# A two-layer decode kernel: spacing of the MLP steps, 24 instead of 48 streamed copies, evictions split evenly

## The chip, the cores and the metric

The kernel runs on one core of a Trainium2 chip. The metric is the device time of one execution in microseconds (us), lower is better. PE is the matmul engine (TensorE), with PEld its weight loads; DVE is VectorE, ACT is ScalarE, POOL is GpSimd. "Clock" is the TensorE clock that the throttle granted, as a share of full speed; the records show it at 1.0 or 0.5, and means in between.

## The reference, cut to what matters

Four blocks run in turn on 8 rows (batch 8, one token each, D = 448): attention, MLP, attention, MLP. Both attention blocks read the same K and V caches.

```
k_cache, v_cache: (8 rows, 8 kv heads, 4096, 256) bf16;  16 query heads
x = x + attention(layernorm(x))      # softmax(q k^T / 16) v, then @ wo (4096 x 448)
x = x + B(layernorm(x))              # x1 = x + ...; x1 + gelu(layernorm(x1) @ w3) @ w4
... the same two once more, same weights
```

With one token a row, the shifted convolution inside B reads only padding, so w1 and w2 drop out. What remains is 480 MB of loads, nearly all K and V (the kernel keeps the transposed K of four of a row's eight heads from layer 0 to layer 1), and little arithmetic on each byte.

## The kernel before

One row's layer 1 can start only when its layer 0 and the small dense work between (output projection, layernorm, w3, gelu, w4, layernorm, new queries: here "the MLP") are done. So the kernel interleaves: attention heads go one after the other, and the MLP of the row that has just finished layer 0 is cut into steps which are put between the attention pieces. A Python generator yields once per step. 47 of a row's 70 steps issue matmuls (8 or 7 of them); the other 23 issue a few tiny VectorE operations, or nothing.

```
def pump():                                   # called at every slot
    credit["n"] = credit["n"] + credit["rate"] if jobs else 0.0     # rate 0.8
    while credit["n"] >= 1.0:
        credit["n"] -= 1.0
        step()                                # next(jobs[0])

def mix(lo, n, then_q, ...):                  # one row: n = 1
    for c in range(KC):
        for t in range(0, 32, 8):
            outputs(lo, n, c, range(t, t + 8), t == 0, True)   # c = 0 has 64-wide weights
            yield                             # 16 TensorE steps
    yield from layernorm(...)                 # 7 steps, VectorE
    scaled(lnT, r_ln, 1, n)
    ...
    yield
    yield
    for t in range(0, NF, 2):
        project(w3_cols, w3_r, C_H, t, t + 2, n)
        yield                                 # 7 TensorE steps
    ...                                       # gelu 3, w4 8 TensorE steps, then queries:
                                              # layernorm 7, two empty, 16 TensorE steps, copy to qT
```

A head that streams K calls `turn(f)` eight times (4 transposes of 128x128 f32 on PE into one PSUM bank, then an eviction of 128x512 on DVE or ACT), `score(f)` eight times (8 matmuls, K as the weight), and multiplies by V twice (16 matmuls each). There is a slot after each turn, six of the scores and each V half: 16 slots a head. Between the end of a row's layer 0 and its layer 1 lie 95 slots; what is left by then is issued at once (`drain`).

```
# a projection with one vector (n = 1) streams it repeated, 48 columns wide:
def copies(cols, n):
    return cols.unsqueeze(1).to_broadcast([cols.shape[0], 2 * N_REP // n, n])   # N_REP = 24
ON_ACT = (2, 5, 7)                # of the eight evictions of a head, these go to ScalarE
```

K and V come in chunks of 1 MiB through a ring of 5 slots (K half, K half, V half, V half of the head before). PE frees a K half after four turns, so a late PE leaves the DMA queue without a free slot.

## Time and profile before

| | before |
|---|---|
| time | 1244.03 us (1243.63 to 1244.42, 2 runs) |
| PE busy, PEld busy | 81%, 72% |
| DVE, ACT busy | 544 us, 269 us |
| mean clock | 0.912 |
| loaded | 480 MB, 386 GB/s over the span |

The first fence has lines of the profile page: the span, PE's busy time, and the rows of 40 equal slices (clock in tenths, GB/s).

```profile
span 1245.7 us, 42311 instructions
...
PE 1008.9 (81%) x19176; PEld 894.5 (72%) x19176; DVE 544.1 (44%) x1785; ACT 268.8 (22%) x811; POOL 105.5 (8%) x281
...
PEclk9888998899988998899888999899888998999995
...
GB/s 351 382 415 419 389 383 399 416 384 389 406 414 420 336 385 409 412 389 385 399 417 416 364 387 420 416 384 367 417 412 386 385 398 413 418 381 375 394 391 89
```

DMA reaches 415 to 420 GB/s in some slices and falls below 390 in others, in every row's period. The view by windows shows one such place, where a row's MLP steps begin (head at 399). The columns are each engine's busy us (instructions), then clock, DMA share, GB/s.

```profile
core 0: us, PE busy (x) PEld busy (x) DVE busy (x) ACT busy (x) POOL busy (x), PEclk, DMA share, GB/s
395.00:400.00 5.00, 1.54 (x21) 1.22 (x22) 0.67 (x3) 0.76 (x4) 0.61 (x2) 0.81 1.02 421
400.00:405.00 5.00, 5.00 (x42) 4.17 (x41) 1.69 (x5) 0.59 (x1) 0.00 (x0) 0.50 1.00 415
405.00:410.00 5.00, 5.00 (x78) 4.75 (x78) 1.34 (x2) 0.59 (x1) 0.00 (x0) 0.67 0.77 279
410.00:415.00 5.00, 5.00 (x117) 4.38 (x116) 1.63 (x6) 1.17 (x5) 0.36 (x1) 1.00 0.57 182
415.00:420.00 5.00, 5.00 (x97) 4.93 (x96) 3.19 (x9) 1.35 (x4) 0.48 (x2) 1.00 0.99 372
```

PE is mostly idle up to 399 (1.54 us busy of 5), then all of each window is busy, at half clock at first; from 405 on the loads starve (279 and 182 GB/s). That the ring is full then is read from the code.

Two pieces of the timeline of PE (start us, span us, what), both at full clock, show what a step costs.

```profile
545.64 0.50 PE L428 MATMUL mm<-oT,wo_sb 128*128 128x48 bf16 x8
545.98 0.62 PE L562 MATMUL tk<-ident,ring 128*128 128x128 f32 x4
...
1195.09 0.34 PE L476 MATMUL mm<-hT,w_sb 128*128 128x42 bf16 x7
1195.27 0.36 PE L586 MATMUL ps<-qT,ktr 128*128 128x48 bf16 x8
```

From the start of a step to the start of what follows: 8 matmuls that stream one element 48 times take 0.34 us (42 ns each); 7 that stream 7 different elements, 42 columns in all, take 0.18 us (26 ns each).

Last, three of PE's waits for DVE (us in total, times, longest us): for the layernorm result (lnT, or t, which follows it), and for the new queries.

```profile
PE mm L399 <- DVE lnT L372: 8.1, 10, 3.0
PE mm L399 <- DVE t L372: 5.0, 1, 5.0
PE ps L586 <- DVE qT L415: 0.7, 1, 0.7
```

About 5.0 and 3.0 us of these are waits at the very end and the very start.

### The profile page before, as it was taken

To read this page: it belongs to the slowest core of one execution; us is meant where nothing else is said; L and a number is where in the kernel's file an instruction comes from. 1 tells how busy PE (TensorE), PEld (TensorE's weight loads), DVE (VectorE), ACT (ScalarE), POOL (GpSimd) and SP (SyncE) were. 2 spreads that over 40 slices of the span, in tenths; PEclk is the share of its full clock that TensorE was granted. 3 is DMA by queue.
4 is the path that set the end of the run, shared out by engine and by line. 5 is a ranking of instruction groups with operands and counts; after the bars stand their busy time and mean duration, and the time that the engine had idled before them with its cause. 6 is when DMAs were issued, how large, how long until landed. Compare 5 with 4: busy or idle time off the path is not lost.

```text
span 1245.7 us, 42311 instructions
## 1 busy us (share of the span) xinstructions
PE 1008.9 (81%) x19176; PEld 894.5 (72%) x19176; DVE 544.1 (44%) x1785; ACT 268.8 (22%) x811; POOL 105.5 (8%) x281
## 2 busy tenths in 40 slices
PE   4577897788877897788877887889778888789785
PEld 4567786677766886677766876778677877688674
DVE  3334553346333453345334543445333643445352
ACT  0222222222222221222221222222222222212120
POOL 0000000000010000100110010000100000000100
PEclk9888998899988998899888999899888998999995
DMA  9999999999999899999999999999999999999992
GB/s 351 382 415 419 389 383 399 416 384 389 406 414 420 336 385 409 412 389 385 399 417 416 364 387 420 416 384 367 417 412 386 385 398 413 418 381 375 394 391 89
DMA packets 71668, 483.06 MB, mean 388 GB/s; under 512 B 7344, under 2 KB 13248, under 8 KB 13696
## 3 DMA queue, kind: packets, MB, share of 16 engines
q1 hardware_dynamic: 71488, 480.36, 96.3%
q8 instruction: 150, 2.46, 0.8%
q14 instruction: 30, 0.25, 0.0%
HBM read 480.32 MB, written 0.01 MB: 386 GB/s over the span
## 4 chain that ended last, share of the span: by engine, by line
PE 52%; DMA 32%; DVE 11%; issue 4%; POOL 1%; ACT 0%; SPq 0%; POOLq 0%; DVEq 0%; ACTq 0%
DMA ring<-in_A_k_cache_dram 30%; PE tk L562 25%; PE ps L586 9%; PE mm L399 6%; PE mm L428 4%; PE pvb L656 3%; DVE ktr L569 3%; DMA ring<-in_A_v_cache_dram 2%; PE mm L476 2%; PE pvb L674 2%; DVE sm L333 1%; DVE sm L334 1%; DVE sm L351 1%; POOL gm L632 1%; DVE sm L332 1%
## 5 line engine op out<-in xcount | busy, mean ns | idle before, releaser
L562 PE MATMUL tk<-ident,ring 128*128 128x128 f32 x3072 | 531.0, 306 | 113.1 <-DMA ring<-in_A_k_cache_dram 111.4
L562 PEld LDWEIGHTS tk<-ident,ring 128*128 128x128 f32 x3072 | 377.0, 156 | 136.1 <-DMA ring<-in_A_k_cache_dram 129.8
L569 DVE COPY ktr<-tk 128x512 f32<-128x512 f32 x320 | 218.1, 689 | 209.0 <-PE tk L562 207.3
L656 PE MATMUL pvb<-ring,pT 128*2 128x256 bf16 x4096 | 158.2, 274 | 53.2 <-DMA ring<-in_A_v_cache_dram 49.5
L567 ACT COPY ktr<-tk 128x512 f32<-128x512 f32 x192 | 112.5, 586 | 367.9 <-PE tk L562 367.9
L586 PE MATMUL ps<-qT,ktr 128*128 128x48 bf16 x4096 | 178.1, 184 | 14.3 <-DVE ktr L569 11.8
L586 PEld LDWEIGHTS ps<-qT,ktr 128*128 128x128 bf16 x4096 | 156.4, 97 | 32.0 <-DVE ktr L569 19.0
L569 DVE COPY keep<-tk 128x512 f32<-128x512 f32 x160 | 109.8, 691 | 149.8 <-PE tk L562 149.6
L586 PEld LDWEIGHTS ps<-qT,keep 128*128 128x128 bf16 x4096 | 149.5, 99 | 26.0 <-issue 19.7
L586 PE MATMUL ps<-qT,keep 128*128 128x48 bf16 x4096 | 159.5, 186 | 6.2 <-issue 5.3
L638 ACT ACTIVATE pT<-ps,nb 128x32 bf16<-128x32 f32 x256 | 76.7, 300 | 296.0 <-DVE nb L634 283.9
L656 PEld LDWEIGHTS pvb<-ring,pT 128*2 128x2 bf16 x4096 | 74.7, 82 | 81.1 <-DMA ring<-in_A_v_cache_dram 60.7
L632 POOL PARTITION_ALL_REDUCE gm<-pm x128 | 45.7, 357 | 873.2 <-DVE pm L629 873.2
L567 ACT COPY keep<-tk 128x512 f32<-128x512 f32 x96 | 56.3, 587 | 272.7 <-PE tk L562 272.7
L629 DVE TENSOR_REDUCE pm<-ps 128x2 f32<-128x64 f32 x128 | 28.7, 224 | 143.7 <-PE ps L586 143.7
L662 DVE COPY ob<-pvb 128x256 f32<-128x256 f32 x128 | 53.9, 421 | 60.1 <-PE pvb L656 60.0
L428 PE MATMUL mm<-oT,wo_sb 128*128 128x48 bf16 (+5 forms) x1280 | 77.6, 203 | 1.9 <-DVE oT L681 1.9
L399 PE MATMUL mm<-lnT,wq_sb 128*128 128x48 bf16 x1152 | 69.1, 205 | 7.5 <-DVE lnT L372 7.5
L428 PEld LDWEIGHTS mm<-oT,wo_sb 128*128 128x128 bf16 (+1 forms) x1280 | 62.9, 105 | 12.5 <-issue 6.1
L674 PE MATMUL pvb<-ident,ob 128*128 128x128 f32 x256 | 60.3, 323 | 11.8 <-DVE ob L662 11.7
L399 PEld LDWEIGHTS mm<-lnT,wq_sb 128*128 128x128 bf16 x1152 | 55.9, 99 | 13.8 <-DVE lnT L372 9.6
L643 POOL PARTITION_ALL_REDUCE dn<-rs x128 | 51.3, 401 | 151.5 <-ACT pT L638 151.5
(59 smaller groups left out, 402.5 us busy)
## 6 DMA issues: line engine op xcount, KB each, us to landing
ring<-in_A_v_cache_dram SPq DMA_DIRECT2D x256, 1024.0 KB, 9.7
ring<-in_A_k_cache_dram SPq DMA_DIRECT2D x192, 1024.0 KB, 9.5
wo_sb<-in_A_wo_dram SPq DMA_DIRECT2D x1, 3584.0 KB, 23.0
wq_sb<-in_A_wq_dram SPq DMA_DIRECT2D x3, 1024.0 KB, 14.6
w_sb<-in_B_w_dram SPq DMA_DIRECT2D x1, 1568.0 KB, 20.6
w_sb<-in_B_w_dram SPq DMA_DIRECT2D x3, 448.0 KB, 16.5
wq_sb<-in_A_wq_dram SPq DMA_DIRECT2D x1, 512.0 KB, 11.3
w_sb<-in_B_w_dram SPq DMA_DIRECT2D x1, 224.0 KB, 16.1
```

What stands on the lines that cost most here:

```text
L399: last = e.matmul(room(P, at + t * B, n), cols(kc, t), copies(lnT[:, kc, 0:n], n), start=(kc == 0), stop=(kc == KC - 1), skip_group_check= ...
L428: last = e.matmul(room(w, at, n) if alone else mm[0:w, at:at + n], wo[:, t, row0(c):row0(c) + w], copies(cols, n) if alone else cols, star ...
L562: last = e.transpose(bank[:, j * P:(j + 1) * P], src[:, 4 * (f % 4) + j, :].bitcast(f32), ident4[:, :])
L567: op("act", lambda e: e.copy(flat, bank[:, :]), reads=[r_bank], writes=[r_kt])
L569: op("dve", lambda e: e.tensor_copy(flat, bank[:, :]), reads=[r_bank], writes=[r_kt])
L586: last = e.matmul(pst[:, at:at + 2 * N_REP].rearrange("p (r j) -> p r j", j=2), kt(i, c), repeated(qT[:, b, c, 2 * h:2 * h + 2]), start=(c ...
L632: op("pool", lambda e: e.partition_all_reduce(gm[q][0][:, :], pm[q][0][:, :], P, ReduceOp.max), reads=[pm[q][1]], writes=[gm[q][1]])
L638: return e.activation(pT[q][0][:, :, :].rearrange("p i j -> p j i")[:, j, :], pst[:, C_S:C_S + 2 * NI].rearrange("p (i j) -> p j i", j=2)[ ...
L643: op("pool", lambda e: e.partition_all_reduce(dn[q][0][:, :], rs[q][0][:, :], P, ReduceOp.add), reads=[rs[q][1]], writes=[dn[q][1]])
L656: last = e.matmul(pvb[at:at + 2, 0:DH], pT[q][0][:, a * HALF + i, :], v[:, i, :], start=(a == 0 and i < 4), stop=(a == 1 and i >= HALF - 4 ...
L662: op("dve", lambda e: e.tensor_copy(ob[:, :], pvb[:, 0:DH]), reads=[r_pv], writes=[r_ob])
L674: last = e.transpose(pvb[:, DH + c * P:DH + (c + 1) * P], ob[:, c * P:(c + 1) * P], ident4[:, :])
```

## The change

Its intent: spread a row's MLP steps over all 95 slots, with steps that cost PE time further apart than steps that don't; make the repeated vector half as wide; give ScalarE half the evictions.

```
+N_MLP = 24
 def copies(cols, n):
-    return cols.unsqueeze(1).to_broadcast([cols.shape[0], 2 * N_REP // n, n])
+    return cols.unsqueeze(1).to_broadcast([cols.shape[0], N_MLP // n, n])
 def room(w, at, n):
-    r = 2 * N_REP // n
+    r = N_MLP // n
 ...
     def step():
         if jobs:
+            n = len(S.ops["pe"])
             try:
                 next(jobs[0])
             except StopIteration:
                 jobs.pop(0)
+            return 1.0 if len(S.ops["pe"]) > n else 0.4
+        return 1.0
 
     def pump():
-        credit["n"] = credit["n"] + credit["rate"] if jobs else 0.0
-        while credit["n"] >= 1.0:
-            credit["n"] -= 1.0
-            step()
+        credit["n"] = min(1.0, credit["n"] + credit["rate"]) if jobs else 0.0
+        if credit["n"] > 0.0:
+            credit["n"] -= step()
 ...
-    ON_ACT = (2, 5, 7)
+    ON_ACT = (1, 3, 5, 7)
 ...
-            credit["rate"] = 0.8
+            credit["rate"] = 0.62
```

Stepping through both rules by hand for the 70 steps (P a TensorE step, d another, . an empty slot) gives these slots:

```
before .PPPP.PPPP.PPPP.PPPP.dddd.dddd.dPPP.PPPP.dddP.PPPP.PPPd.dddd.dddd.dPPP.PPPP.PPPP.PPPP.Pd
after  PP.PP.P.PP.PP.P.PP.PP.P.PdddddddddPPP.PP.P.PdddPPP.P.PP.PP.ddddddddddPPP.PP.P.PP.PP.P.PP.PP.P.d
```

## The prediction

> **What bounds it now.** The DMA queue table shows 480 MB; at the best rate that 5 us windows hold for long (I use 420 GB/s) that is 1144 us, and some 21 us of tail follow (timeline: attention ends at 1225, the span at 1245.7). So about 75 us are lost transfer. A row's period is 140 us (chain of waits: 249.7, 386.3, 528.1), though its 52 chunks of 1 MiB need 130. DMA's busy share (0.96) hides it; the GB/s column shows it. In the windows of one row it sags while that row's MLP steps run, 402 to 463 us: 279 and 182 GB/s at 405-415, 328 to 359 at 430-440, 445-450 and 455-460; from 465 to 545 it is 401 to 426 but for one window of 346. In most of the sagging windows PE is 5.0 of 5.0 busy: ring slots come free late.
>
> **PE's account.** Warm, a streamed head takes PE about 6.9 us without MLP steps (454.75 to 464.39 less 8 steps); its 4 chunks take DMA 10.0 us. An MLP step of 8 matmuls, one vector in 48 copies, takes 0.34 us (42 ns each) in the timeline; at 0.8 steps in each of 16 slots that is 4.35 us, 11.2 in all: over 10. Each row begins cold (granted clock 0.50, 0.67 in 400-410): a step takes 0.56 us, a transpose group 0.85 to 1.04.
>
> **What the change does.**
> 1. 24 copies: the scores (48 columns in pairs) run at about 26 to 32 ns a matmul, and the MLP steps with 7 distinct columns (42 wide) at 0.18 us for 7, 26 ns. So one repeated element seems to stream slowly, and 24 should reach that floor: about 0.21 us a step (estimate). The Trainium skill, "TensorE: Matmul & The Clock Gate", "Back-to-back issue gap", gives one floor of about 25 ns for 1 to 64 columns; the trace agrees for pairs and not for the single repeated element. 47 TensorE steps a row: about 6 us less PE.
> 2. Spacing: TensorE steps fall from 0.8 to 0.62 per slot; the others stay near one. By my count 70 steps need 88 slots before and 95 after, and 95 are there, so nothing is left to drain. MLP load per head: 16 x 0.62 x 0.21 = 2.1 us, 9.0 in all: under 10.
> 3. Evictions: DVE loses one of eight (689 ns) and ACT gains one (586 ns); they alternate. DVE waits in a row's layernorm stretch shrink; perhaps 1 us a row.
>
> **How much is critical.** Warm, PE no longer exceeds DMA; the cold start of each row (about 4.5 us of lost transfer in 405-415) shrinks to about 2. I expect 3 of the 10 us lost per row to stay: 7 x 7.5 rows is about 52 us, less 1 to 2 us in the tail.
>
> **Predicted: 1193 us, 8 in 10 within 1174 to 1217.** Chances: faster by over 2% 0.90, within 2% 0.09, slower 0.01.
>
> **What would show it.** Row period 132 to 134 us; GB/s over 390 in nearly every slice; MLP matmuls 25 to 28 ns start to start when warm; PE busy falls by 40 to 60 us; chain with more DMA and less PE; ACT near 325 us, DVE near 478.
>
> **What would make it wrong.** PE stays cold in row starts because steps are sparser and narrower; the 24-copy matmul keeps 42 ns; steps are left over and drained at once, stalling a row; DMA cannot hold 420 GB/s through a whole row.

## The result, and the profile after

After: 1230.62 us (1230.51 to 1230.72, 2 runs) against 1244.03; ratio 0.9892, interval 0.985 to 0.9935. It is faster, but by 1.1%, and outside the range predicted. Ratios in this document are the mean time of one kernel's fast runs over that of the other's in the same rounds, so not quite the ratio of the medians.

The lines of the page that answer to those of before:

```profile
span 1228.8 us, 42309 instructions
...
PE 983.8 (80%) x19176; PEld 866.1 (70%) x19176; DVE 485.9 (40%) x1689; ACT 324.5 (26%) x907; POOL 105.4 (9%) x281
...
GB/s 345 378 416 420 410 413 418 415 409 418 415 418 405 366 402 420 420 364 404 414 416 372 404 384 421 419 363 379 403 423 374 403 414 419 409 354 411 410 370 106
```

From the third to the twelfth slice the loads hold 409 to 420 GB/s: two whole rows run as predicted. From the thirteenth on, each row has a slice or two between 354 and 384. The same place by windows, row head at 389:

```profile
385.00:390.00 5.00, 1.84 (x31) 1.42 (x28) 0.89 (x4) 0.76 (x4) 0.76 (x2) 0.76 1.01 421
390.00:395.00 5.00, 4.52 (x38) 3.72 (x37) 1.73 (x4) 0.59 (x1) 0.00 (x0) 0.50 1.00 421
395.00:400.00 5.00, 5.00 (x68) 4.41 (x67) 0.69 (x1) 1.10 (x2) 0.00 (x0) 0.50 0.94 360
400.00:405.00 5.00, 5.00 (x111) 4.35 (x111) 1.56 (x6) 1.06 (x5) 0.36 (x1) 0.87 0.41 120
405.00:410.00 5.00, 5.00 (x113) 4.93 (x112) 2.31 (x5) 2.11 (x5) 0.40 (x1) 1.00 1.02 416
```

The clock stays at half for all of 390 to 400, and the loads fall to 120 GB/s. The timeline of PE (start us, span us, what, idle before and what ended it) shows the start of that stretch, and below the dots a step at full clock:

```profile
389.01 1.97 PE L566 MATMUL tk<-ident,ring 128*128 128x128 f32 x8 [2.12 <-DMA ring<-in_A_k_cache_dram]
390.77 0.63 PE L678 MATMUL pvb<-ident,ob 128*128 128x128 f32 x2
391.88 0.61 PE L429 MATMUL mm<-oT,wo_sb 128*64 128x24 bf16 x8 [0.48 <-DVE oT L685]
392.42 1.11 PE L566 MATMUL tk<-ident,ring 128*128 128x128 f32 x4
...
406.06 0.37 PE L429 MATMUL mm<-oT,wo_sb 128*128 128x24 bf16 x8
406.27 0.36 PE L590 MATMUL ps<-qT,ktr 128*128 128x48 bf16 x8
```

A warm step of 8 matmuls now takes 0.21 us (406.06 to 406.27), as predicted. At half clock a step with the 64-wide weights takes 0.54 us (391.88 to 392.42), where before, in 48 copies, it took 0.56. And the first step, which stands in the first slot, waits 0.48 us for DVE (oT, the attention output that it multiplies).

Three of PE's waits for DVE have grown:

```profile
PE mm L400 <- DVE lnT L373: 15.6, 10, 2.2
PE ps L590 <- DVE qT L416: 9.5, 9, 1.1
PE mm L400 <- DVE t L373: 8.5, 9, 5.0
```

They sum to 33.6 us, against 13.8 before (8.1 + 5.0 + 0.7). Others shrank, those for evicted K (ktr) from 11.8 to 3.4 us and for the V result (ob) from 11.7 to 6.1, so that all of PE's waits for DVE together stayed as they were (53.3 us before, 54.6 after; 42.8 in c24_evict below, which lacks the spacing). What changed is where PE waits.

A measure for each row helps to read what follows. A row's head is the head in which its MLP steps begin; its start is read in the timeline (399.07 before, 389.01 after). The row period is the distance of two heads. From 1-us windows I counted those with a clock under 0.75 from 1 us ahead of the head to 16 us behind it ("cold").

| | cold us at the 8 row heads | row periods, us |
|---|---|---|
| before | 0, 3, 9, 0, 5, 4, 6, 3 | 137.0, 138.1, 140.5, 137.0, 137.8, 137.7, 138.5 |
| after | 0, 0, 12, 10, 10, 10, 10, 13 | 132.1, 132.2, 136.6, 137.1, 137.6, 139.0, 135.6 |

In the changed kernel, rows that start warm take 132 us, as predicted; rows that start cold take 136 to 139. The two warm rows have the grown waits too (for lnT 1.4 and 0.9 us, for qT 1.1 us each), and their periods do not show them. A row's loads, 52 chunks of 1 MiB, would need 130 us at 420 GB/s.

### The profile page after: what moved, and what is told of

Its sections match the earlier page's. It is cut to its first block, busy times and chain, and to the rows that moved or that the text cites. A ratio compares the mean times of both kernels' runs of the same rounds, so it can differ in the third digit from the quotient of the medians.

```text
span 1228.8 us, 42309 instructions
## 1 busy us (share of the span) xinstructions
PE 983.8 (80%) x19176; PEld 866.1 (70%) x19176; DVE 485.9 (40%) x1689; ACT 324.5 (26%) x907; POOL 105.4 (9%) x281
## 4 chain that ended last, share of the span: by engine, by line
PE 49%; DMA 38%; DVE 8%; issue 4%; POOL 1%; ACT 0%; SPq 0%; POOLq 0%; DVEq 0%; ACTq 0%
DMA ring<-in_A_k_cache_dram 35%; PE tk L566 26%; PE ps L590 10%; PE pvb L660 4%; PE mm L429 3%; PE mm L400 3%; DMA ring<-in_A_v_cache_dram 2%; DVE ktr L573 2%; PE pvb L678 2%; PE mm L477 1%; DVE sm L334 1%; DVE sm L335 1%; DVE sm L352 1%; POOL gm L636 1%; DVE sm L333 0%
## 5 line engine op out<-in xcount | busy, mean ns | idle before, releaser
L566 PE MATMUL tk<-ident,ring 128*128 128x128 f32 x3072 | 544.4, 312 | 117.3 <-DMA ring<-in_A_k_cache_dram 115.6
L566 PEld LDWEIGHTS tk<-ident,ring 128*128 128x128 f32 x3072 | 382.8, 158 | 142.4 <-DMA ring<-in_A_k_cache_dram 137.1
L573 DVE COPY ktr<-tk 128x512 f32<-128x512 f32 x256 | 176.6, 690 | 225.8 <-PE tk L566 224.2
L571 ACT COPY ktr<-tk 128x512 f32<-128x512 f32 x256 | 150.0, 586 | 352.9 <-PE tk L566 352.9
L573 DVE COPY keep<-tk 128x512 f32<-128x512 f32 x128 | 88.4, 691 | 143.8 <-PE tk L566 143.4
L571 ACT COPY keep<-tk 128x512 f32<-128x512 f32 x128 | 75.1, 586 | 241.2 <-PE tk L566 241.2
L429 PE MATMUL mm<-oT,wo_sb 128*128 128x24 bf16 (+5 forms) x1280 | 64.9, 187 | 7.2 <-DVE oT L685 4.8
L429 PEld LDWEIGHTS mm<-oT,wo_sb 128*128 128x128 bf16 (+1 forms) x1280 | 54.9, 109 | 19.6 <-issue 10.5
L400 PE MATMUL mm<-lnT,wq_sb 128*128 128x24 bf16 x1152 | 51.0, 183 | 14.0 <-DVE lnT L373 14.0
L400 PEld LDWEIGHTS mm<-lnT,wq_sb 128*128 128x128 bf16 x1152 | 43.3, 98 | 18.7 <-DVE lnT L373 16.3
```

Of the source, the lines that this page charges most:

```text
L400: last = e.matmul(room(P, at + t * B, n), cols(kc, t), copies(lnT[:, kc, 0:n], n), start=(kc == 0), stop=(kc == KC - 1), skip_group_check= ...
L429: last = e.matmul(room(w, at, n) if alone else mm[0:w, at:at + n], wo[:, t, row0(c):row0(c) + w], copies(cols, n) if alone else cols, star ...
L566: last = e.transpose(bank[:, j * P:(j + 1) * P], src[:, 4 * (f % 4) + j, :].bitcast(f32), ident4[:, :])
L571: op("act", lambda e: e.copy(flat, bank[:, :]), reads=[r_bank], writes=[r_kt])
L573: op("dve", lambda e: e.tensor_copy(flat, bank[:, :]), reads=[r_bank], writes=[r_kt])
```

## The experiments

Each call of runs had its own chip and its own runs of the kernel before (median 1238 to 1242 us), so ratios are the safer comparison.

| kernel | median us (range, runs) | ratio to before (95%) | cold us at the 8 row heads |
|---|---|---|---|
| only_24 | 1213.41 (1204.34 to 1221.97, 4) | 0.9800 (0.9749 to 0.9851) | 0, 0, 4, 10, 4, 4, 4, 3 |
| only_space | 1278.98 (1275.35 to 1285.89, 4) | 1.0312 (1.0276 to 1.0348) | 10, 10, 10, 6, 7, 10, 7, 10 |
| only_evict | 1234.90 (1231.81 to 1237.21, 4) | 0.9948 (0.9926 to 0.9970) | 0, 3, 6, 0, 6, 0, 4, 10 |
| after_48 | 1262.64 (1254.39 to 1264.66, 4) | 1.0161 (1.0124 to 1.0198) | 0, 7, 7, 0, 0, 10, 6, 10 |
| after_warm | 1211.30 (1210.14 to 1212.53, 4) | 0.9747 (0.9715 to 0.9780) | 0, 0, 0, 0, 0, 0, 0, 1 |
| after_warm_late | 1254.34 (1251.84 to 1256.53, 4) | 1.0093 (1.0057 to 1.0129) | 0, 13, 13, 13, 13, 12, 10, 13 |
| before_warm | 1239.69 (1238.04 to 1241.32, 4) | 0.9973 (0.9932 to 1.0014) | 0 at all eight |
| c24_evict | 1206.88 (1202.33 to 1207.77, 4) | 0.9711 (0.9673 to 0.9748) | 3, 3, 0, 12, 4, 4, 4, 0 |
| c24_evict_warm | 1205.05 (1202.77 to 1206.36, 4) | 0.9701 (0.9667 to 0.9736) | 0 at all eight |
| after_dve_packed | 1256.51 (1255.25 to 1261.33, 4) | 1.0127 (1.0080 to 1.0174) | 7, 7, 10, 10, 0, 11, 11, 0 |
| after_pe_sparse | 1217.82 (1216.03 to 1218.91, 4) | 0.9805 (0.9770 to 0.9839) | 7, 10, 10, 10, 0, 6, 0, 10 |
| after_late_start | 1208.13 (1204.30 to 1216.18, 4) | 0.9740 (0.9698 to 0.9781) | 3, 3, 4, 4, 6, 0, 0, 0 |
| after_c0_last | 1219.71 (1212.53 to 1221.73, 4) | 0.9814 (0.9777 to 0.9851) | 0, 7, 9, 0, 7, 3, 7, 7 |
| packed_gap | 1219.42 (1215.95 to 1219.98, 4) | 0.9816 (0.9793 to 0.9840) | 0, 7, 11, 13, 13, 10, 0, 7 |
| after_end_early | 1215.27 (1210.86 to 1219.10, 4) | 0.9777 (0.9745 to 0.9809) | 0, 10, 11, 7, 10, 10, 10, 12 |
| new_late_gap | 1208.66 (1199.56 to 1214.61, 6) | 0.9754 (0.9710 to 0.9797) | 0, 14, 3, 13, 6, 6, 13, 3 |
| old_late | 1204.74 (1201.78 to 1206.48, 6) | 0.9723 (0.9694 to 0.9751) | 0, 0, 13, 3, 4, 0, 6, 6 |
| new_gap_warm | 1205.08 (1202.84 to 1206.84, 5) | 0.9724 (0.9702 to 0.9746) | 11, then 0 at seven |

All gave correct results. The changed kernel itself stands at 0.9892. The cold counts are those of the one profiled execution of each kernel.

### First round: the parts one by one

My theory after reading the result was that narrower and sparser steps keep PE at half clock where a row starts. The rival was that the amount of PE work there decides.

only_24: the kernel before with `N_MLP = 24` in `copies` and `room`, and nothing else.

> The kernel before with 24 copies alone. Cold-start theory (the row starts lose transfer because PE is at half clock, and narrow MLP steps keep it there): warm MLP steps fall to about 0.21 us, but more rows start cold, gain only 5 to 10 us (1234 to 1239). Rival (what is lost at row starts comes from the amount of PE work, not from the clock): at least 12 us gained, under 1232.

It gained 2.0%, so the narrower steps are no burden: the first form of my theory fell here, and the rival's number held. Its four runs went together with the mean clock: 1204 and 1209 us at 0.913 and 0.909, 1222 and 1218 at 0.889 and 0.890.

only_space: the kernel before with the new `step` and `pump` and rate 0.62 alone.

> The kernel before with the new spacing alone, 48 copies. Cold-start theory: sparser steps also leave PE more waits, gain 3 to 8 us (1236 to 1241). Rival (amount of work per slot decides): 4.35 us of MLP a head fall to 3.4, gain about 8 to 15 us.

Both theories had expected a gain; it lost 3.1%. This is the finding of the round: **the spacing, meant to help, costs.** Seven of its eight rows start cold for 7 us or more, and PE's waits for DVE grow as in the changed kernel:

```profile
PE mm L399 <- DVE lnT L372: 19.4, 10, 3.0
PE mm L399 <- DVE t L372: 13.2, 9, 5.0
PE ps L589 <- DVE qT L415: 9.6, 9, 1.1
```

only_evict: `ON_ACT = (1, 3, 5, 7)` alone.

> The kernel before with the evictions split in half alone. Both theories: DVE busy falls by 66 us, ACT rises by 56, the time by 0 to 5 us (1239 to 1244).

It gained 0.5% (6 us by the medians), just more than both theories said.

after_48: the changed kernel with `N_MLP = 48`.

> The changed kernel with 48 copies again. Cold-start theory: fewer cold row starts and shorter ones, but warm stretches lose more; about the same as the changed kernel, 1225 to 1236. Rival (amount of work): slower than the changed kernel by 8 us or more, 1238 or above.

It lost 1.6% against before, as the rival said: with the new spacing the wide steps are worse, not better. The three parts do not add up (-2.0, +3.1 and -0.5 sum to +0.6%, and all together give -1.1%): with cheaper steps the spacing costs less.

### Second round: is it the clock at the row starts?

after_warm: 96 matmuls with an unused result fill PE's wait ahead of each row's head (rows 1 to 7; row 0 has none).

```
+ def filler(g):                      # 48 columns each, into a free part of the score bank
+     for _ in range(96):
+         last = e.matmul(ps[g % N_PS][0][:, 256:256 + 2 * N_REP], ident[:, :], ident[:, 0:2 * N_REP],
+                         start=True, stop=True, ...)
  def attend(g):
+     if <g - 2 is the last head of layer 0 of a row b > 0>: filler(g)
```

> The changed kernel with 96 idle-filling matmuls of 48 columns (about 2.5 us warm, result unused) put into PE's wait ahead of the head in which a row's MLP steps begin. Cold-start theory: the row starts run warm, each of some 6 rows gets back about 3 us of transfer, 1208 to 1217. Rival (the loss at row starts comes from the work there): nothing gained or 1 to 3 us lost, 1230 to 1234.

1211.30 us, in the range of the cold-start theory. No row starts cold, and the loads no longer collapse. The windows of the same row (head at 390.7), against 360 and 120 GB/s above:

```profile
386.00:391.00 5.00, 3.95 (x139) 3.52 (x132) 0.89 (x4) 0.79 (x5) 0.75 (x2) 1.00 1.01 416
391.00:396.00 5.00, 4.52 (x68) 3.67 (x67) 1.74 (x4) 1.17 (x2) 0.00 (x0) 1.00 1.01 419
396.00:401.00 5.00, 5.00 (x136) 4.52 (x134) 1.61 (x3) 1.17 (x2) 0.00 (x0) 1.00 0.92 310
401.00:406.00 5.00, 5.00 (x106) 4.81 (x99) 2.92 (x8) 1.93 (x6) 0.75 (x2) 1.00 0.98 369
```

So added work made the kernel 19 us faster, since it holds the clock up. The first step still waits 0.5 us for oT in every row, and the waits for lnT, t and qT are as long as before (15.4, 8.5 and 9.4 us), so none of these is what was gained.

after_warm_late is the control: the same 96 matmuls three heads later.

> Control: the same 96 matmuls three heads later in the row, in the MLP stretch, where the clock is mostly up. Both theories: no gain, 1230 to 1240; the row starts stay cold.

24 us slower than the changed kernel by the medians: the filling does not help by itself, only where it bridges the wait, and PE time inside the MLP stretch is paid for (7 fillings of 2.5 us are 17.5 us). Its profiled run has one more cold row start than that of the changed kernel (seven of eight). My range had allowed for 10 us.

before_warm: the kernel before with the filling at row heads.

> The kernel before with the same filling at row starts. Cold-start theory: only about 1 of its rows starts an MLP stretch cold, so little to win, 1238 to 1246. Rival: same or slower, 1244 to 1250.

Not separable from no change (0.9973, interval to 1.0014). All its row starts are warm, so in the kernel before there was nothing to gain there that outweighs the filling; by only_24, most of its loss lies in the dear 48-copy steps.

### Third round: what in the new spacing?

c24_evict: the changed kernel with the old `step`, `pump` and rate 0.8.

> The changed kernel with the old spacing (24 copies, half the evictions on ScalarE). Since the spacing alone cost 38 us and 24 copies alone gained 27: if the spacing costs with 24 copies too, 1203 to 1215, 15 to 27 us faster than the changed kernel; if it only hurts with 48 copies, 1226 to 1234.

1206.88 us: undoing the spacing makes the changed kernel 1.8 percentage points faster. Its row periods are 132.2, 132.5, 132.3, 135.8, 132.3, 132.8 and 132.5; the long one follows the one head that was cold for 12 us.

c24_evict_warm: the same with the filling.

> The same with the 96 filling matmuls at row starts: the candidate for the fastest. Cold-start theory: 4 to 10 us under the kernel without them, and a narrower spread, 1196 to 1206. Rival (the spread and loss left have another cause): no better.

1205.05, with no cold row start: 1.8 us better at the median, less than expected and inside the spread.

after_dve_packed: the changed kernel with rate 0.8 in place of 0.62. TensorE steps are about as dense as before; the runs of VectorE steps stay unbroken, 9 and 10 slots, as in the changed kernel, but fall in other slots of the heads.

> The changed kernel at the old rate of 0.8 for TensorE steps, with the other steps still one per slot (78 slots in place of 95). If packed VectorE steps are what the new spacing costs: still 1220 to 1235, PE's waits for lnT still over 20 us in all. If sparse TensorE steps and the flush end are what it costs: 1203 to 1215.

1256.51, the slowest of the kernels with 24 copies, and worse than my range for "packed steps are the cost". The timeline of DVE and PE at the end of a layernorm shows why:

```profile
425.39 0.18 DVE L373 TENSOR_TENSOR lnT<-xc,sm 128x4 bf16<-128x4 f32 x1
425.47 0.16 DVE L373 TENSOR_TENSOR t<-xc,sm 128x4 f32<-128x4 f32 x1
425.62 0.39 PE L400 MATMUL mm<-lnT,w_sb 128*128 128x24 bf16 x8 [2.78 <-DVE t L373]
425.95 1.02 PE L660 MATMUL pvb<-ring,pT 128*2 128x256 bf16 x16
```

Packed into 9 slots, the layernorm's chain of some 25 tiny DVE operations (0.2 us each) ends after PE has come to the first matmul that reads it. PE idles 2.78 us; then the clock is down, and 16 V matmuls take 1.02 us where warm ones take 0.61. In six of its eight rows PE is cold in three places while MLP steps run (at the head and after each layernorm); over the whole run that makes 358 us cold (253 in the changed kernel).

after_pe_sparse: the changed kernel with TensorE steps at 0.68 a slot and a cost of 0.77 for the others, so about 0.88 a slot, still 95 slots.

> The changed kernel with TensorE steps at 0.68 a slot and the other steps at about 0.88, 95 slots again (ends flush with the next layer). If sparse TensorE steps and the flush end are the cost: 1220 to 1235, with PE's wait for the queries' copy near 9 us. If packed VectorE steps are: 1205 to 1216.

1217.82: between the two answers and near the second. By the ratios, this gives back 0.9 of the 1.8 points (0.9892, 0.9805, 0.9711), though not by the packing alone, as TensorE steps are denser too (0.68 a slot against 0.62); row starts are still cold (five of eight for 7 us or more), and the wait for the queries is still 9.3 us.

### Fourth round: mechanism by mechanism

after_late_start: the first step of a row later, rate 0.66.

```
-            credit["rate"] = 0.62
+            credit["rate"] = 0.66
+            credit["n"] = -3 * 0.66
```

> The changed kernel with a row's first MLP step three slots later and a rate of 0.66 (94 slots, so it still fits). If the clock fails to rise because MLP steps thin out PE's work in the first 3.4 us or so of the head: most rows start with 4 us or less at half clock, 1210 to 1219. If the start does not matter: rows stay cold for about 10 us, 1225 to 1233.

By rounding, the credit is a hair over zero in the third slot, so the step comes two slots later, not three. 1208.13 us: no row start is cold for more than 6 us. (Its layernorm waits are longer than the changed kernel's, 16.1 and 15.8 us against 15.6 and 8.5, so they are not what was gained. But PE's wait for the queries, 9.5 us there, fell to 0.7 us here, since the steps end two slots sooner; the 22 us are not the row starts' alone. after_warm, which kept that wait at 9.4 us, gives them 19.)

after_c0_last: `for c in (1, 2, 3, 0)` in the output projection, so that the 64-wide weights come last.

> The changed kernel with the output projection's 64-wide part last in place of first; the work is the same. If the slow 64-wide weight loads keep the clock down at row starts: most rows warm within 4 us, 1210 to 1219. If not: 1226 to 1233.

1219.71: 11 us gained, just short of the 12 to 21 that I had expected. Cold starts shorten from 10 us or more to 3 to 9 us. So the slow narrow loads play a part, but are not the whole.

packed_gap: the packed kernel with four more empty slots after each layernorm.

```
         yield
         yield
+        yield
+        yield
+        yield
+        yield
         for t in range(0, NF, 2):        # and the same in queries
```

> The packed kernel (after_dve_packed, 1256 us) with four more empty slots after each layernorm, before the matmuls that read it: the packing stays, PE's wait of 2.8 and 1.5 us for the layernorm result goes. If that wait and the cold stretch behind it are the cost: 1212 to 1232. If packed VectorE steps cost by delaying evictions: 1245 to 1258.

1219.42 against 1256.51: 37 us come back with the packing left in place. What remains of PE's two waits is the one at the start and the one at the end:

```profile
PE mm L400 <- DVE t L373: 5.0, 1, 5.0
PE mm L400 <- DVE lnT L373: 3.9, 1, 3.9
```

So it is the wait for the layernorm, with the cold stretch behind it, and not the load of DVE as such. This holds for waits of 2.8 and 1.5 us a row; those of the changed kernel are about half as long.

after_end_early: the changed kernel with rate 0.68, 89 of 95 slots.

> The changed kernel at a rate of 0.68, so that a row's steps end 6 slots before the next layer (89 of 95): PE's wait for the queries' copy (9.5 us in all) goes. If that wait counts: 1218 to 1226. If it lies where PE has slack: 1227 to 1236.

1215.27, below my range. The wait for the queries went (0.7 us left), but the waits for the layernorm fell too (lnT 15.6 to 6.5, t 8.5 to 5.0), as the steps landed in other slots; the run cannot say which of the two gave the 15 us. Row starts stayed cold, yet rows cold for 7 to 11 us took 133.8 to 135.3 us here, against 135.6 to 139.0 in the changed kernel: the waits seem to cost where a row starts cold and PE has no time to spare, and not in a warm row (one execution of each).

### Fifth round: do the two costs make up the whole?

new_late_gap: late first step (`credit["n"] = -3 * 0.7`), two more empty slots after each layernorm, rate 0.7.

> The changed kernel with both costs taken away: the first MLP step of a row two slots later, two more empty slots after each layernorm, rate 0.7 (94 of 95 slots). If the two explain the loss: 1196 to 1207, no slower than the old spacing with 24 copies (1207). If sparser steps cost something more: 1208 to 1218.

Two groups: three runs at 1199.56, 1203.33 and 1204.15 (clock 0.905 to 0.908), three at 1213.17 to 1214.61 (0.887 to 0.891). The profiled run is of the slower group and has three rows with 13 or 14 us cold. The median lies in the range of the second answer, but by the split and not by a common cost. A later start makes the cold row start rarer, not impossible.

old_late: c24_evict with the first step two slots later (`credit["n"] = -2 * 0.8`).

> The old spacing with 24 copies and half the evictions on ScalarE, first MLP step of a row two slots later (90 of 95 slots). Only about one of its rows starts cold for long, so 2 to 5 us at most: 1201 to 1207.

1204.74, inside the range; not separable from c24_evict (0.9723 against 0.9711).

new_gap_warm: new_late_gap with the filling.

> new_late_gap with the 96 filling matmuls ahead of each row's first MLP head. If cold row starts are the whole split: no row cold at its start, all runs within about 5 us of each other, 1196 to 1205. If something else is left: still two groups of runs, one of them above 1210.

Five runs within 4 us, 1202.84 to 1206.84: the split is gone. Only row 0, which has no filling, starts cold (11 us). So cold row starts were the whole split, and without them and without the layernorm waits the new spacing is as fast as the old one with 24 copies (0.9724 against 0.9711), not faster.

No version beats c24_evict by more than the spread; c24_evict, c24_evict_warm, old_late and new_gap_warm share first place at about 1205 us, 2.8 to 3.0% under the kernel before. The simplest of them is the change without its spacing.

### Why a cold start lasts 4 us or 12

One row in c24_evict with 4 us cold: PE's timeline, then its clock in windows of 1 us.

```profile
656.87 1.97 PE L563 MATMUL tk<-ident,ring 128*128 128x128 f32 x8 [1.87 <-DMA ring<-in_A_k_cache_dram]
658.63 0.63 PE L675 MATMUL pvb<-ident,ob 128*128 128x128 f32 x2
659.06 0.87 PE L563 MATMUL tk<-ident,ring 128*128 128x128 f32 x4
659.86 0.44 PE L429 MATMUL mm<-oT,wo_sb 128*64 128x24 bf16 x8
```

```profile
658.00:659.00 1.00, 1.00 (x6) 1.00 (x6) 0.69 (x1) 0.12 (x1) 0.00 (x0) 0.50 0.94 393
659.00:660.00 1.00, 1.00 (x10) 0.83 (x9) 0.39 (x3) 0.47 (x1) 0.00 (x0) 0.70 1.04 434
660.00:661.00 1.00, 1.00 (x25) 0.89 (x24) 0.66 (x1) 0.00 (x0) 0.00 (x0) 1.00 1.00 418
```

The head opens with 3 us of nothing but transposes, one behind the other, and the clock is back near 659.6, just ahead of the first MLP step. In the changed kernel the first step comes sooner, and PE stands still 0.48 us for DVE ahead of it. The Trainium skill, "TensorE: Matmul & The Clock Gate", Part 1, says that the clock is set by how busy PE was in free-running windows of about 3.4 us. The counts above, 3 to 4, 7, 10 and 13, agree with steps of that size. That the dense opening is what lifts the clock in time fits after_late_start and after_c0_last.

The clock records inside the kept traces hold the phase of these windows too. In each of the 20 traces the clock changes only on a fixed grid of 3.41 us. Sorted by PE's busy share in one window, full clock was followed by half clock in 520 of 520 cases under 40%, in 329 of 1366 between 40 and 75%, and in 5 of 3764 from 75% on. Near row heads (from 3.4 us ahead to 13 behind), half clock was followed by full clock in 48 of 48 windows with PE busy for 98% or more and no 64-wide step, in 43 of 97 with 64-wide steps, and in 0 of 38 where PE was busy for less and 64-wide steps ran. In five of the changed kernel's six cold rows the window with the first step is only 86 to 88% busy, with the wait of 0.48 us in it; the next one is full, but holds 64-wide steps. By these counts, how the grid happens to fall on the 3 us of transposes decides between 4 us and 12. This is a count over the traces, with modelled ends of matmuls, and not an experiment; after_c0_last comes nearest to one.

## Why the prediction was wrong

**What bounds the kernel: right.** Loads lost because ring slots come free late. Where the loss went, the row period fell to 132 us, the predicted 132 to 134.

**Step 1, 24 copies: right.** 0.21 us a warm step, as estimated; alone it gave 2.0%. PE busy fell by 25 us and not 40 to 60, in part since at half clock the rest takes longer (the transposes of K went from 531 to 544 us).

**Step 2, spacing: wrong, and this is the step that failed.** The prediction said that TensorE steps would "fall from 0.8 to 0.62 per slot; the others stay near one", and that 95 slots are there, "so nothing is left to drain". It counted PE's load per head and not what each step waits for. Alone the spacing cost 3.1%; with the other two parts, 1.8 points (0.9892 against 0.9711). Most of that is one thing: the first step in the first slot, with a wait for DVE, at heads where the clock is down (19 us by after_warm). Two more can cost: unbroken runs of VectorE steps, which PE outruns (shown in the large by packed_gap, 37 us, where the waits are about twice as long), and no slack at the end (9.5 us of wait for the queries). In the changed kernel their share by themselves stayed open, and it is small once the heads are warm: after_warm keeps both and stands at 0.9747 against 0.9711 for c24_evict, with overlapping intervals. The costs overlap and don't sum.

**Step 3, evictions: right in size.** DVE 485.9 us and ACT 324.5, against 478 and 325 predicted; worth 0.5% alone.

**The cold start: wrong in direction.** I wrote "Each row begins cold" from one row, that at 399, which turned out the worst of eight. I expected the 4.5 us that it loses to shrink to 2. Rows of the changed kernel that start cold lose about 4 us of transfer (1-us windows, shortfall against 420 GB/s), and six of eight do so, where before it was one for 9 us and none longer. "PE stays cold in row starts because steps are sparser and narrower" was listed among what could go wrong, with too little weight; narrower was not the reason (only_24), and with steps nearly as sparse (0.66) that begin two slots later no row was cold for more than 6 us (after_late_start).

The prediction cited the one floor of about 25 ns for narrow matmuls. The runs agree with it at 24 copies (26 ns).

## What to carry to other kernels

Work that is spread between the pieces of another chain must be placed by what it waits for, not only by what it costs: a packed chain of small vector operations ahead of a matmul turns into a wait on the matmul engine. A wait can also cost later: here some 3 us of waiting for loads ahead of a row head could be followed by half clock and about 4 us of lost transfer, so a version that keeps the clock down for longer can lose most of what its cheaper work gained. When three edits go in together, run each alone: here one of the three was taking away more than half of what the others gave.

## What the Trainium skill lacked or had wrong

- "TensorE: Matmul & The Clock Gate", "Back-to-back issue gap", gives one floor for 1 to 64 columns. A single element repeated 48 times took 42 ns a matmul, 7 different elements in 42 columns 26 ns, one element repeated 24 times 26 ns, two elements in turn over 48 columns (the scores) 26 ns (0.21 us for 8, after_end_early at 562.74). That the pattern of the streamed operand matters is missing.
- The same page's table of advice warns of idle gaps over about 3 us. Here no gap was that long, but two came close together, with 0.6 us of work between: 1.04 and 1.87 us (656.9 in c24_evict, 4 us cold) or 1.03 and 2.09 us (521.1, 12 us) took the clock to half, while 1.05 and 1.87 us left it up elsewhere (539.6 before). Shorter gaps that add up are a risk too.
- Part 4 of that page says that transposes don't count as busy for the clock in the same way, and that full clock does not engage for them. In c24_evict it rose from 0.50 to 1.0 near 659.6 after 3 us in which PE ran f32 transposes alone.
- The page's section "Weight-path perf modes" ties fast weight loads to 128 weights; the runs fit that and give a size: with 24 copies a warm step of 8 matmuls takes 0.37 us with 64-wide weights and 0.21 with 128-wide ones.
- "DMA: Bandwidth & Descriptors", Specifications, lists about 358 GB/s as the limit of one core's loads without a condition; only the page's later section on bandwidth says that this is the share with both cores of a pair at work, and that one alone reaches more. Here one core held 415 to 426 GB/s in many windows of 5 us, so the table's line taken alone would mislead.
